# Two layers of linear attention and gated MLP: the sum of the two halves moved to TensorE in the first two tiles, under a newly searched order

## The chip, the cores and the metric

The kernel runs on one core of a Trainium2 chip. A core has TensorE (PE in the profile, with its weight loads as PEld), VectorE (DVE), ScalarE (ACT), GpSimd (POOL) and SyncE (SP), which here only issues transfers; 16 DMA engines move data. TensorE multiplies a stationary block of up to 128x128 with a moving block of up to 512 columns and writes to PSUM. The other engines take their operands from PSUM or from the on-chip memory SBUF. Each engine works through its own list of instructions in order, and waits at an instruction until the semaphores that it names have counted far enough. The metric is the time of one execution on the device, in microseconds (us).

## The reference

The input x has 2048 tokens of 512 channels in bf16. Four stages follow one another, attention A and MLP B, twice, with the same weights:

```
x = x + A(layernorm(x));  x = x + B(layernorm(x));  x = x + A(layernorm(x));  x = x + B(layernorm(x))

A: q, k, v = layernorm(x) @ wqkv            32 heads of 16 channels
   phi(u)  = concat(softmax(u w), softmax(-u w))     per head, w = w_phi
   kv = sum over tokens of phi(k) v^T;  z = sum over tokens of phi(k)
   o  = phi(q) kv / (phi(q) z + 1e-6);  A = o @ wo
B: h  = relu(y @ W_gate) * (y @ W_up)       1376 columns;  B = h @ W_down
```

phi has two halves, one from the softmax of u w and one from that of -u w, so o is a sum of two products, one for each half. Attention is linear: kv and z are sums over all tokens, so the keys of all tiles must be through before the first tile's o can be made.

## The kernel before, in words

The 2048 tokens are 16 tiles of 128. The line numbers are those of the kernel before; in the changed kernel the same code stands 201 lines higher, since a table of numbers became shorter (L867 becomes L666).

For each layer the following is done. Keys, per tile: statistics of x (L810, L811), their logarithm and exponential for the inverse deviation (L818, L820), the normalized tile (L825) and its transpose, by TensorE with an identity and an evacuation for the first tiles, and by a DMA transpose from SP for the others (`turn`, L785 to L805). Then K and V on TensorE (L849, L855), two exponentials on ScalarE (`ek`, L852), their sums per head on VectorE (`sk`, L860), logarithm and exponential of the sums for their inverse (L867, L870), the product phi (L879, on VectorE or GpSimd), and its product with V (`kvz`, L896), which is summed over the 16 tiles in PSUM. From this sum VectorE builds R, the right-hand side of the queries (L918, L924). Queries: TensorE makes Q for four tiles at a time (L937), ScalarE its two exponentials (`Eq`, L941).

Attention, per tile (`attend`, L947): TensorE multiplies Eq with R (`erq`, L955), ScalarE or VectorE copies numerators N and denominators DS out of PSUM, VectorE makes the weights w of the two halves (L971 to L977) and the products pr (L980), adds the two halves to o (L985), o is transposed (`oT`), TensorE projects it (L992), and VectorE adds it to x (L1001). For the first two tiles of a layer the last addition also leaves the row sum of x (L997), so that the centring for the MLP (L1018) doesn't wait for the statistics. In these two tiles transposes are made by TensorE (L797) and evacuated by ScalarE or VectorE; in the others they are DMA transposes.

MLP, per block of one to four tiles (`mlp`, L1006): gate and up on TensorE (L1068, the last 96 columns at L1044), relu and copy out of PSUM (L1072, L752, L753), their product hT (L1076), down on TensorE (L1101) and the addition to x (L1108). The next layer's keys of a tile start when its MLP is done.

Which instruction comes when is not in this text. Every operation is put in a list with its engine, a cost, what it depends on and which buffers it takes. `arrange` and `plan` (L71 on) then go through a model of the five engines and put the instructions in order: of those that can start at the earliest time on an engine, the one with the smallest number in the table DUE goes first. DUE has one number for each operation; it was found by a random search (annealing), not written by hand. A second table of 301 bits, PLACE, says for each PSUM evacuation and each phi product whether it moves to its other engine (ScalarE or VectorE; VectorE or GpSimd). The order is fixed in the built program; at run time the waits alone decide. Where the model has TensorE idle before the first kvz, filler matmuls of zeros are put in (`idle`, L744).

The step that the change touches in `attend` is chosen by a flag:

```
if how == "SP" or not SUM_ON_PE:      # o = pr[0] + pr[1] on VectorE, then turn(o)
else:                                 # turn(pr, parts = its two halves)
```

With two parts, `turn` issues for each of the four blocks of 128 columns two matmuls into the same PSUM columns, the first with start, the second with stop, so that PSUM holds the transposed sum.

Of the kernel before, what the change touches and what calls it, by code (L numbers as in the profile page):

```python
# [226 lines left out]
class K:  # L227
# [9 lines left out]
    "1101000110000001001100001000100000000000010001111000011000010001110001000000000000011100100010111111"  # L237
    "1111000010110100000100000010000001100000011001011000011111100010000100001101010000001001111011010000"
    "1111100110100000010110000100000010100000010011011010100001000001001010001111110011001101111011000111"
# [4 lines left out]
SUM_ON_PE, SPLIT, SUMMED = False, False, 2  # L244
# [6 lines left out]
    124840698555718, 124252925051631, 124840698555715, 125332623046249, 125332623046237, 125332623044945,  # L251
    124563716811943, 124651474002544, 125330408190868, 125332623046304, 124563716811957, 126266507667699,
    125634454115563, 126229628066192, 121775727240306, 126167001450013, 126167001450460, 127129188121561,
    127129188120464, 127094235901023, 126466639653490, 130976565015723, 126315242830809, 126026073780216,
    127094235902555, 127129188121381, 126296162928321, 126296162928067, 124164240787164, 125426364192401,
    125402334135098, 125572680463274, 125519371767392, 125974726071829, 125750504763376, 125579757280012,
    125111116517781, 125262546662859, 123870973169851, 125479091639646, 125519634893654, 125402750569735,
    125720420032606, 126315242829367, 126115429498044, 125777194724969, 125402334135128, 125288327727618,
    125426364192382, 125079834957741, 125262546664085, 125297196294117, 125083742970748, 125572680463271,
    125682458895960, 125340531910116, 125650771760537, 124924227899641, 125375805988896, 125375805988747,  # L260
    125222585690632, 124164240787379, 125079834952887, 125682458896453, 125073457285470, 124441555417783,
    125262546664362, 124559450906168, 125312265963603, 125309490505260, 125650771760388, 125521196029889,
    125302414876135, 125288971855969, 125302414876075, 125319036718893, 125310924577113, 125301244472799,
    125319889098234, 125304622980711, 124441555417022, 124696086271192, 125037102060107, 125289095968268,
    125310342882178, 125097433264852, 123938863413234, 125098635011495, 125302414877679, 125298443103361,
    125302414877834, 125345179807080, 125281974922696, 125170893464912, 125310924577844, 125298773455122,
    124760528650159, 125079834956090, 124164240787032, 125519634912639, 125297196294120, 125289095970570,
    125112530384860, 124947956071454, 125087041208877, 125295339242047, 125295339242044, 125310342881683,
    125302414876836, 125563590222055, 124550413597701, 125170893460583, 125310439811694, 125310924578485,
    125310342891023, 125079834956128, 125059086062919, 125340531910042, 125288971857093, 124938480631522,  # L270
    125016964293686, 125288327733509, 125223398503866, 125345179804453, 125223398503371, 125223398503413,
    128002429020973, 125310342881575, 125004873625443, 125004873624115, 125304250990101, 125307858833262,
    126406478372943, 124715538660738, 125381551257299, 125298773455119, 125309931740009, 125034120871986,
    125223398503145, 124934003878247, 124920547621783, 125117660356287, 125304250989589, 125381551258296,
    125724846491348, 125381551257440, 125381551255756, 124974964922671, 125098650067446, 125291692659804,
    125289095968030, 125289095968469, 125345179805242, 125288327732492, 125098635010687, 125281974923160,
    125307858833059, 125223398502787, 125307858834522, 125140858237361, 126040889629027, 125223398503832,
    125364446854524, 125252231261123, 125381551257841, 125304250990712, 125381551257935, 125172912230709,
    124370185364736, 125108599924050, 125310339518705, 125302251176246, 125291692659817, 116464344164560,
    124922363544296, 125116688267329, 125108599923765, 125310109452139, 125303189236999, 125098650066178,  # L280
    125111066291136, 125026249417504, 125310339519068, 125302251175868, 125301748943397, 125307858834419,
    125262656080157, 125307858833334, 125307858831723, 125281974922936, 125016007547146, 125096908962168,
    125140858236352, 126184070097670, 126789461067573, 124985972327150, 126493631750672, 125298443105832,
    125108599921161, 125095405692172, 124194527561572, 123915330190996, 125076395401661, 125296253501352,
    125034337760696, 125310144379949, 125172912227871, 124207139224249, 123569728375339, 125298628392740,
    125302384093186, 125034337760404, 125310109456339, 125302384093798, 124931075024483, 125294295865377,
    125294295865373, 125302251176101, 125315738277133, 125311054768224, 126406478373023, 125172912230494,
    125096908962530, 125251794872554, 124920547622585, 125303189240357, 125098650068694, 119253338445520,
    125310144376109, 124936451836160, 123979775168383, 123985197582245, 125308558845483, 125268086740942,
    125296661283390, 125310109454666, 125308302113579, 124976494725716, 125154886386050, 125154886386047,  # L290
    125310339518837, 125310339520186, 125311054773229, 115427298652791, 125028606409972, 125308302117330,
    124740066372422, 125309837287326, 124971491447171, 125390463209015, 125414317459497, 124998168317548,
    125310257912136, 125310339399315, 123124172544908, 125030291594481, 125098650066121, 125251794874681,
    125098650067377, 118590723041837, 125302384093189, 118558518521843, 119253338445444, 125315738276049,
    106461658784164, 94447193084223, 125174401625687, 125154442634399, 124740066371701, 125309837288789,
    124971491447250, 125700597007401, 125308302114021, 125724451257015, 125310339520700, 125310339519418,
    125311054772244, 106461658774504, 124207139226908, 125192403773820, 124998168316146, 125311054772195,
    124441758064121, 124971491449373, 125317969331587, 125317969332560, 124974964922433, 121939852109137,
    121830280691129, 125172912227838, 125310144376073, 124836416131697, 125170954590710, 125294295865680,
    125251220555668, 124971491446350, 133210835393138, 125310144376062, 159383179923936, 115427298651984,  # L300
    124869899796944, 121608346900103, 125317969331111, 124895461028154, 124971491450562, 122185707429267,
    122708677636727, 123917343997726, 121939852110706, 123578599439449, 125019087637949, 159383179924917,
    115648665651868, 116063440630281, 125317969332636, 125074078432251, 125317969331341, 123519743654385,
    125310236008505, 120537880156542, 118420113792879, 123578599438633, 121692118966927, 159383179923941,
    159383179924147, 127715336141955, 159383179924206, 127715336141958, 106461658780311, 125332623047314,
    126229643281022, 124563716811954, 124651474004320, 125262546664382, 125310498011902, 125304250992350,
    125345179806077, 125297457021900, 125309490506988, 125310342881875, 125650771760502, 125311152414122,
    125301606200720, 121534934577895, 125301606200572, 125341707123588, 121534934577391, 125311152414125,
    121534934577404, 125652646373752, 125303189240274, 125381551256039, 125304250990207, 125170893460707,
    125170893460683, 125136322776291, 125281974922790, 125098635010684, 125298443103066, 125170893464861,  # L310
# [909 lines left out]
```

The softmax here doesn't subtract the row's maximum and nothing guards it: scores larger than these inputs give would overflow.

## Time and profile before

The time is the median of three runs. The profiled run took 383.81 us, of which the profile spans 382.0.

| | before |
|---|---|
| time, median of 3 (lowest to highest) | 383.95 us (383.66 to 384.04) |
| span of the profiled execution | 382.0 us, 7622 instructions |
| TensorE busy | 371.5 us (97%) |
| VectorE busy | 311.1 us (81%) |
| ScalarE busy | 215.0 us (56%) |
| GpSimd busy | 41.9 us (11%) |
| sum of halves on VectorE (L985) | 32 instructions, 413 ns each |
| transposes of o on TensorE (L797) | 16 matmuls of 128 columns |
| granted TensorE clock | full in all 40 slices |

Busy time is the time in which an engine has at least one instruction under way. Successive instructions of VectorE and ScalarE overlap a little in their records, so that the durations of an engine's instructions add up to more than its busy time. A line of a stretch (A:B) gives its length and then, for each engine, busy us and in brackets the number of instructions. A line of the waits says which engine waited for which engine's line, then us in total, number of waits, and the longest. A line of the timeline gives start and length in us, engine, line, operation, output and inputs, and in square brackets the idle time just before it with what ended it.

### The profile page before, as it was taken

To read this page: it belongs to the slowest core of one execution; us is meant where nothing else is said; L and a number is where in the kernel's file an instruction comes from. 1 tells how busy PE (TensorE), PEld (TensorE's weight loads), DVE (VectorE), ACT (ScalarE), POOL (GpSimd) and SP (SyncE) were. 2 spreads that over 40 slices of the span, in tenths; PEclk is the share of its full clock that TensorE was granted. 3 is DMA by queue.
4 is the path that set the end of the run, shared out by engine and by line. 5 is a ranking of instruction groups with operands and counts; after the bars stand their busy time and mean duration, and the time that the engine had idled before them with its cause. 6 is when DMAs were issued, how large, how long until landed. Compare 5 with 4: busy or idle time off the path is not lost.

```text
span 382.0 us, 7622 instructions
## 1 busy us (share of the span) xinstructions
PE 371.5 (97%) x2787; PEld 224.4 (59%) x2832; DVE 311.1 (81%) x798; ACT 215.0 (56%) x554; POOL 41.9 (11%) x44
## 2 busy tenths in 40 slices
PE   7999998999989999999999999999999999999996
PEld 4545456967545445554656654696855544467575
DVE  7999999999999989983694677999998976763334
ACT  6999989636445316772455679984526412243040
POOL 0276710000200000230020124000000000000000
PEclk9999999999999999999999999999999999999999
DMA  8497720222221321211200100013322221020110
GB/s 232 122 205 219 188 89 2 52 58 62 57 56 41 44 54 40 45 23 27 45 6 15 22 8 1 2 36 70 77 44 70 57 56 56 14 62 16 41 50 29
DMA packets 60869, 22.83 MB, mean 60 GB/s; under 512 B 52672, under 2 KB 59808, under 8 KB 60832
## 3 DMA queue, kind: packets, MB, share of 16 engines
q1 hardware_dynamic: 60416, 21.95, 24.9%
q8 instruction: 22, 0.36, 0.4%
q10 hardware_dynamic: 416, 0.39, 0.4%
q14 instruction: 15, 0.12, 0.1%
HBM read 7.91 MB, written 2.10 MB: 26 GB/s over the span
## 4 chain that ended last, share of the span: by engine, by line
PE 77%; DVE 17%; DMA 2%; issue 2%; ACT 1%; DVEq 0%
PE b L1068 31%; PE b L1101 17%; PE b L855 5%; PE b L849 5%; PE b L992 5%; PE b L937 5%; PE q L955 3%; PE b L1044 2%; PE q L896 2%; DMA xnTA<-xn 2%; DVE pr L980 1%; DVE bstA L810 1%; DVE bstB L810 1%; DVE sk L860 1%; DVE N L753 1%
## 5 line engine op out<-in xcount | busy, mean ns | idle before, releaser
L1068 PE MATMUL b<-xnTB,wgu 128*128 128x128 bf16 (+2 forms) x1191 | 152.3, 279 | 0.5
L1068 PEld LDWEIGHTS <-wgu 128*128 128x128 bf16 x1200 | 97.7, 98 | 42.5
L1072 ACT ACTIVATE gu<-b 128x512 bf16<-128x512 f32 (+1 forms) x83 | 48.0, 584 | 63.7 <-PE b L1068 61.3
L1101 PE MATMUL b<-wd,hT 128*128 128x512 bf16 (+3 forms) x349 | 82.3, 372 | 0.7
L879 POOL TENSOR_TENSOR phiK<-ek,sk 128x512 bf16<-128x512 bf16 x38 | 41.2, 1102 | 192.3 <-ACT sk L870 164.1
L1101 PEld LDWEIGHTS <-hT 128*128 128x128 bf16 (+1 forms) x363 | 34.7, 98 | 33.9 <-DVE hT L1076 0.2
L1076 DVE TENSOR_TENSOR hT<-gu 128x512 bf16<-128x512 bf16 (+1 forms) x83 | 34.0, 414 | 15.4 <-ACT gu L752 14.2
L1108 DVE SCALAR_TENSOR_TENSOR X<-b,rsB,X 128x512 bf16<-128x512 f32 (+1 forms) x33 | 23.7, 729 | 23.8 <-PE b L1101 23.8
L752 ACT CAST gu<-b 128x512 bf16<-128x512 f32 (+1 forms) x50 | 28.4, 570 | 24.0 <-PE b L1068 20.4
L860 DVE TENSOR_REDUCE sk<-ek 128x64 f32<-128x1024 bf16 x32 | 38.6, 1210 | 2.7 <-ACT ek L852 2.3
L852 ACT ACTIVATE ek<-b 128x512 bf16<-128x512 f32 x64 | 36.0, 616 | 8.3 <-PE b L849 8.1
L941 ACT ACTIVATE Eq<-b 128x512 bf16<-128x512 f32 x64 | 37.3, 629 | 3.3 <-PE b L937 3.1
L752 ACT CAST N<-q 128x384 bf16<-128x384 f32 (+1 forms) x59 | 26.1, 464 | 12.4 <-PE q L955 6.7
L855 PE MATMUL b<-wv,xnTA 128*128 128x512 bf16 x123 | 31.9, 379 | 0.3
L937 PE MATMUL b<-xnTA,Wq 128*128 128x512 bf16 x125 | 31.9, 379 | 0.2
L849 PE MATMUL b<-Wk,xnTA 128*128 128x512 bf16 x123 | 31.6, 379 | 0.4 <-DVE xnTA L753 0.2
L992 PE MATMUL b<-wo,oT 128*128 128x512 bf16 x120 | 31.3, 379 | 0.4
L753 DVE CAST gu<-b 128x512 bf16<-128x512 f32 (+1 forms) x33 | 21.8, 665 | 11.1 <-PE b L1068 11.1
L955 PE MATMUL q<-R,Eq 128*128 128x144 bf16 x256 | 27.5, 226 | 1.8 <-DVE N L753 1.3
L955 PEld LDWEIGHTS <-Eq 128*128 128x128 bf16 x256 | 20.3, 98 | 13.1 <-issue 2.6
L980 DVE TENSOR_TENSOR pr<-N,w 128x1024 bf16<-128x1024 bf16 x32 | 21.8, 683 | 0.7
L810 DVE BATCH_NORM_STATS2 bstA<-X 128x6 f32<-128x512 bf16 x32 | 21.3, 682 | 1.2 <-DMA X<-in_A_x_dram 1.0
(75 smaller groups left out, 388.9 us busy)
## 6 DMA issues: line engine op xcount, KB each, us to landing
out_dram<-X SPq DMA_DIRECT2D x15, 128.0 KB, 1.7
X<-in_A_x_dram SPq DMA_DIRECT2D x6, 256.0 KB, 3.3
wgu<-in_B_W_gate_dram SPq DMA_DIRECT2D x4, 344.0 KB, 3.4
wgu<-in_B_W_up_dram SPq DMA_DIRECT2D x4, 344.0 KB, 3.5
wd<-in_B_W_down_dram SPq DMA_DIRECT2D x5, 256.0 KB, 3.5
wv<-in_A_wqkv_dram SPq DMA_DIRECT2D x2, 256.0 KB, 4.7
wo<-in_A_wo_dram SPq DMA_DIRECT2D x4, 128.0 KB, 3.1
oT<-o SPq DMA_TRANSPOSE x28, 2.3
```

Of the source, the lines that this page charges most:

```text
L752: both = {"ACT": ("ACT", act(cols), lambda: nc.scalar.copy(out=out_(), in_=in_()), False), "DVE": ("DVE", dve(cols), lambda: nc.vector.ten ...
L849: k = op("PE", mm(4, 512), due, lambda: [nc.tensor.matmul(kp.t[:], lhsT=xnTA[c][:, b, cols], rhs=Wk2[:, b, :], start=(b == 0), stop=(b == ...
L855: v = op("PE", mm(4, 512), due_v, lambda: [nc.tensor.matmul(vp.t[:], lhsT=xnTA[c][:, b, cols], rhs=wv[:, b, :], start=(b == 0), stop=(b == ...
L860: a = op("DVE", SUM16, due, lambda: nc.vector.tensor_reduce(out=sk.t[:, row, :], in_=ek.t[:].rearrange("p g s (h f) -> p (g s h) f", f=DH) ...
L879: e.tensor_tensor(out=ph.t[:].rearrange("p g s (h f) -> p (g s h) f", f=DH)[:, lo:lo + n], in0=ek.t[:].rearrange("p g s (h f) -> p (g s h) ...
L937: q = op("PE", mm(4, 512), due(c, b), lambda b=b, qp=qp: [nc.tensor.matmul(qp.t[:], lhsT=Wq2[:, m, b * P:(b + 1) * P], rhs=xnTA[c][:, m, : ...
L941: done.append(op("ACT", act(512), due(c, b), lambda b=b, s=s, qp=qp: nc.scalar.activation(out=Eq[c][:, b, s, :], in_=qp.t[:], func=AF.Exp, ...
L955: pe.append(op("PE", mm(len(groups), GE), due, lambda ps=ps, groups=groups: [nc.tensor.matmul(ps.t[:, n * GE:(n + 1) * GE], lhsT=Eq[c][:, ...
L992: a = op("PE", mm(4, 512), due + 3, lambda: [nc.tensor.matmul(yp.t[:], lhsT=oT.t[:, b, :], rhs=wo[:, b, :], start=(b == 0), stop=(b == NB ...
L1068: nc.tensor.matmul(ps.t[:, q * W:(q + 1) * W], lhsT=wgu[:, s, b, g * P:(g + 1) * P], rhs=xT.t[:, b, 0:W], start=(b == 0), stop=(b == NB - 1))
L1072: nc.scalar.activation(out=gu.t[:, 0, 0:cols], in_=gp.t[:, 0:cols], func=AF.Relu)
L1101: nc.tensor.matmul(yp.t[:, 0:c1 - c0], lhsT=h.t[:m, f * W + i * P:f * W + (i + 1) * P], rhs=wd[:m, f, c0:c1], start=(f == 0), stop=(f == N ...
```

## The change

SUM_ON_PE becomes true. SUMMED, the number of tiles with the row sum, is 2 in both kernels. PLACE and DUE are replaced by the result of another search, which began from nothing and was short; there are 2101 numbers for 2105, because four additions are gone. The numbers serve for comparison only, so their size means nothing.

```
-    "1101000110000001001100001000100000000000010001111000011000010001110001000000000000011100100010111111"
+    "0000000100000000001000000010000010000000100000110100111010110000110000100000010001000110001101010101"
...
-SUM_ON_PE, SPLIT, SUMMED = False, False, 2
+SUM_ON_PE, SPLIT, SUMMED = True, False, 2
...
 DUE = (
-    124840698555718, 124252925051631, 124840698555715, 125332623046249, 125332623046237, 125332623044945,
...
+    140234, 138986, 141443, 132421, 137184, 136724,
 )
```

In the built programs the instructions of before and after differ in number as follows: additions L985 on VectorE 32 and 28, transposing matmuls L797 56 and 72, filler matmuls 13 and 15, phi products 26 and 29 on VectorE (38 and 35 on GpSimd), evacuations of V 10 and 6 on VectorE (22 and 26 on ScalarE), and smaller shifts of the same kind. On every engine the order is a different one throughout.

## The prediction

> **What bounds the kernel now.** I read the page first, then the waits of TensorE, then tables by stretch, then the timeline where TensorE stands still.
>
> ```profile
> span 382.0 us, 7622 instructions
> PE 371.5 (97%) x2787; PEld 224.4 (59%) x2832; DVE 311.1 (81%) x798; ACT 215.0 (56%) x554; POOL 41.9 (11%) x44
> ...
> 16.00:48.00 32.00, 31.74 (x213) 15.67 (x216) 30.94 (x55) 30.97 (x89) 21.94 (x22) 1.00 0.81 207
> 48.00:54.00 6.00, 5.95 (x69) 3.60 (x69) 5.58 (x14) 5.00 (x14) 0.92 (x1) 1.00 0.39 130
> 54.00:64.00 10.00, 8.40 (x71) 4.96 (x70) 9.03 (x30) 9.83 (x31) 0.00 (x0) 1.00 0.00 0
> 64.00:100.00 36.00, 35.79 (x369) 27.06 (x371) 35.69 (x116) 20.28 (x57) 0.00 (x0) 1.00 0.27 57
> ...
> PE q L955 <- DVE N L753: 1.3, 2, 1.1
> ...
> PE b L797 <- DVE o L985: 1.0, 2, 0.6
> ```
>
> The columns of the stretch lines are busy TensorE, weight loads, VectorE, ScalarE and GpSimd. TensorE is full, but not alone: from 16 to 48 us (layer 0's keys and values) VectorE and ScalarE are full as well, and to 100 us VectorE still is. Only from 160 us on has TensorE room on all sides. It loses time in few places: 54 to 64 us, where the first attention tiles go through, is the largest with 1.6 us.
>
> To see where exactly, I put a ledger beside the trace. TensorE's work is its matmuls in order at the rate of four of 512 columns in 0.86 us; it comes to 369.9 us. Start time less work done is 4.5 at 12 us, 4.6 at 44, 6.0 at 59, 7.45 at 62.5, 7.3 at 99, 8.5 at 107, 8.4 at 233, 9.0 at 238 and 8.8 at the end; 3.3 us follow the last matmul. So 369.9 + 8.8 + 3.3 = 382.0, the span of the profiled run (383.81 timed; the three others have the median 383.95). The steps at 53 to 62 us (2.6), 107 us (1.2) and 237 us (0.6) are what an order can win or lose; the rest is start and tail.
>
> The timeline shows the first step:
>
> ```profile
> 56.14 0.18 ACT L752 COPY DS<-q 128x32 f32<-128x32 f32 x1
> ...
> 56.54 0.22 DVE L971 TENSOR_TENSOR m<-DS 128x64 f32<-128x64 f32 x1
> ...
> 57.74 0.69 DVE L980 TENSOR_TENSOR pr<-N,w 128x1024 bf16<-128x1024 bf16 x1
> ...
> 58.47 0.42 DVE L985 TENSOR_TENSOR o<-pr 128x512 bf16<-128x512 bf16 x1
> ...
> 58.95 0.40 PE L797 MATMUL b<-ident,o 128*128 128x128 bf16 x4 [0.59 <-DVE o L985]
> ...
> 59.38 0.59 ACT L752 CAST oT<-b 128x512 bf16<-128x512 f32 x1
> ...
> 60.02 1.04 PE L992 MATMUL b<-wo,oT 128*128 128x512 bf16 x3
> ...
> 63.86 1.95 PE L1068 MATMUL b<-xnTB,wgu 128*128 128x128 bf16 x32
> ```
>
> One chain: ScalarE's copy of tile 0's sums, five small VectorE steps, the product, the sum of halves, the transpose, its evacuation, the projection; 3.9 us from 56.1 to 60.0.
>
> **What the Trainium skill says.** "TensorE: Matmul & The Clock Gate", part on the extra over 53.3 ns, puts warm matmuls of 128 and 512 columns back to back at 55.6 and 215.7 ns; the trace agrees: four of 512 in 0.86 us, and 72 of 128 in the 4.18 us from 367.25, 58 each. The same page's step on LDWEIGHTS says that only weight loads are pulled ahead and matmuls keep program order, and its table calls ScalarE's and VectorE's queues strict FIFO. So one early instruction that waits holds all behind it; the trace has VectorE's o holding the transposes of L797 and they the erq matmuls behind them. "VectorE: DVE Perf Modes", tier table, gives tensor_tensor on bf16 in SBUF 1224 ns for 2048 elements; no instruction here has that length, and the row of L985 has 413 ns for 512, which I use.
>
> **The change part by part.** The row sum with the residual (L997) stands in both kernels for t below 2, so this half changes nothing. The sum on TensorE takes four adds from VectorE, 4 x 413 ns = 1.65 us, and gives TensorE 16 more matmuls of 128 columns, 16 x 56 ns = 0.9 us. Two more filler matmuls (15 for 13) add 0.43 us, in waits at the start. TensorE's work becomes 371.2. Placement moves a net 2.1 us onto ScalarE, and with the adds gone some 2 us off VectorE. SP issues 101 transposes in both. All this is small. What matters is that nearly every instruction stands in another place.
>
> For that I extend the ledger to VectorE and ScalarE: mean durations of before's rows, less the overlap of successive records (VectorE's records sum to 360.1 us against 311.1 busy, 0.06 each; ScalarE's to 260.1 against 215.0, 0.08 each). Time less work is then, in before, 2.8 for VectorE from 12 to 48 us, and for ScalarE 4.0 at 16 us and 2.0 at 60.
>
> Step 1, keys of layer 0. ScalarE's logarithm (L867) waits for VectorE's sum (L860). In before ScalarE's ledger stands at 19.9 where VectorE's must stand at 20.8 (its tightest, 0.9 apart), and at 41.1 for 39.9. In after it is 13.5 for 15.2, 16.8 for 18.7, and 41.1 for 41.9. With VectorE 2.8 late, the last pair starts ScalarE at 41.9 + 2.8 + 0.1 = 44.8, where before's ScalarE stood at 41.1 + 2.0 = 43.1. So ScalarE is held by 1.6 us. Bounds: 0 (VectorE earlier by as much) and 3 (what both wait for each other adds up).
>
> Step 2, attention entrance. Tile 0's DS and N copies end at ScalarE's ledger 54.0 and 54.3 in before, 56.1 and 56.4 in after: more of the queries' exponentials (L941, 0.63 us each) go ahead. Without step 1: copy at 56.1 + 2.0 = 58.1, m at 58.2, pr done 1.9 later at 60.1, transposes at once (saving the add's 0.42), 8 in 0.46, done 60.65. Evacuation ends 61.4, projection 61.5 to 62.4, residual 63.2, centring 63.85, transpose 63.9 to 64.3, evacuation 65.05; the second tile's projection runs beside it. First gate/up matmuls start 65.7, with 57.6 us of TensorE's ledger done; in before 63.86, with 56.4. What remains is equal (313.6 and 313.5), so 1.85 us later is 1.85 us longer. With step 1 TensorE's offset is 65.7 - 57.6 + 1.6 = 9.7.
>
> Step 3, VectorE-bound stretch to about 130 us. TensorE must wait where VectorE's ledger leads its own most: before +4.4 at TensorE's 127 (offset 8.35, so VectorE's own is 4.0); after +4.3 at 123. After's m starts at 59.8 with step 1, at ledger 53.3: VectorE is 6.5 late, before 3.9. That makes 10.8 at most; it makes 9.7 if VectorE needs no more than it gets. I take 10.3.
>
> Step 4, layer 1's entrance. First erq stands 1.75 us of TensorE work behind the last kvz in both (wait 0.6 as before). The add saves its 0.42, mostly hidden; the centred tile's transpose stands 0.9 us of work behind the projection instead of 1.7, where 1.3 is needed: 0.4 more. Drift as before -0.2. I take +0.7. Bounds 0 and 1.5.
>
> Transfers: a K at TensorE's 25.1 needs a DMA transpose whose source VectorE makes 1.0 before it in the ledger; the tightest of before is 1.5, with a wait of half a microsecond. That costs up to 0.5, which step 2's ScalarE hides. Tail: the last G/U group is followed by 18 half-width down matmuls (25 mixed in before); the last chunk's copies and product end just before their turn. No change.
>
> Sum: 371.2 + 10.3 + 0.7 + 3.3 = 385.5 of span, 3.5 over before; 383.95 + 3.5 gives 387.4.
>
> **The rivals.** First, not slower: the saved add pays. Place: the transposes of L797 at both entrances; price: 4 x 0.42 = 1.7 off the chains, less 0.9 of TensorE, gives 383.2. It decides if the first gate/up matmul starts by 63.9. For it: the waits on o are TensorE's own. Against: ScalarE, not the add, sets when tile 0's chain starts. Chance 0.13.
>
> Second, worse: in the keys' stretch VectorE waits for ScalarE's exponentials (L852) and ScalarE for VectorE's sums, and each loses what the other lost. If 16 tiles lose 0.2 us each, 3.2 on top of mine: 390.6. For it: three engines at 97% or more leave no slack. Against: the leads grow no further after 18.8. Chance 0.19.
>
> Third, within the main case: VectorE's 2 us less work gives step 3 back, 386.8. I count it there.
>
> **How the numbers follow.** Main case 0.68, at 385.0 to 389.5. A measurement tells about 0.2%, 0.77 us. Below 383.2 lies half of the first rival, 0.06; within 0.2% the other half and an edge of mine, 0.08; slower 0.86. The range leaves out most of the first rival and the upper end of the second: 384.6 to 391.5.
>
> **What would show it.** Step 1: ScalarE's logarithms (L666 in after) wait for the sums more than the 5.7 us of before, and busy ScalarE in 16 to 48 us falls below 30. Step 2: first gate/up matmuls at 66 to 68 us. Step 3: TensorE waits 0.5 us or more on VectorE between 100 and 140 us. Step 4: about a microsecond lost near 240. From 145 to 235 no loss. I am wrong if gate/up starts by 64, or if much is lost after 145.

## The result, and the profile after

The changed kernel takes 387.19 us (median of 4 runs, 386.94 to 388.83), the kernel before, measured beside it, 383.81 (4 runs, 383.61 to 384.04). The ratio is 1.0097, 95% interval 1.0069 to 1.0126: slower by about 1%. The profiled execution spans 385.4 us, 3.4 more than before; 387.4 and 385.5 were predicted.

The head of the page and the stretches, in the columns of the prediction, and below them the stretch from 100 us in before:

```profile
span 385.4 us, 7717 instructions
PE 376.9 (98%) x2850; PEld 225.3 (58%) x2850; DVE 306.6 (80%) x795; ACT 220.2 (57%) x556; POOL 40.7 (11%) x41
...
16.00:48.00 32.00, 30.61 (x213) 14.92 (x212) 30.77 (x53) 30.80 (x87) 16.15 (x15) 1.00 0.93 196
54.00:64.00 10.00, 8.82 (x77) 5.03 (x74) 7.89 (x25) 9.60 (x25) 0.00 (x0) 1.00 0.00 0
...
100.00:160.00 60.00, 59.91 (x356) 30.61 (x355) 56.11 (x161) 29.92 (x75) 4.23 (x4) 1.00 0.25 52
```
```profile
100.00:160.00 60.00, 58.61 (x353) 30.85 (x357) 57.44 (x153) 29.39 (x77) 2.43 (x3) 1.00 0.23 45
```

TensorE's busy time is longer overall; part of that is that the trace of before lacks 45 records of matmuls (2787 for 2832 weight loads). And yet TensorE is idle where it was not before: 1.4 us of the 32 in the keys of layer 0, against 0.3. The last two columns are the share of time in which the DMA engines were busy, and GB/s; in the keys the share is 0.93 for 0.81 before. Between 100 and 160 us, where before lost 1.4, it now stands still for 0.1.

In 20 to 50 us no matmul of before waits for anything; one weight load waits for a transpose:

```profile
PEld L855 <- DMA xnTA<-xn: 0.5, 1, 0.5
```

The waits of the changed kernel's matmuls there, then the queue of SP and TensorE's timeline around the longest:

```profile
PE b L648 <- DMA xnTA<-xn: 1.4, 2, 1.1
```
```profile
25.59 0.58 SPq L473 DMA_DIRECT2D wgu<-in_B_W_up_dram  x1
26.21 0.43 SPq L473 DMA_DIRECT2D wgu<-in_B_W_gate_dram  x1
26.74 1.19 SPq L586 DMA_TRANSPOSE xnTA<-xn  x1
```
```profile
29.42 0.67 PE L695 MATMUL q<-vext,phiK 128*128 128x65 bf16 x16
31.22 1.04 PE L648 MATMUL b<-Wk,xnTA 128*128 128x512 bf16 x4 [1.13 <-DMA xnTA<-xn]
```

K of a tile waits until 31.22 us for a transpose that SP issued at 26.74, directly behind two weight loads. The loads take 4.1 and 4.4 us to land, so they are there at about 29.7 and 30.6, and the transpose lands behind them, at 31.2. The detail of the tile xnTA gives the time from issue to landing of layer 0's twelve transposes, first in before, then in the changed kernel:

```profile
DMA to landing us min/median/max: 2.4/3.1/4.1
```
```profile
DMA to landing us min/median/max: 2.4/3.5/5.4
```

The chain through the first tile, as the prediction showed it for before:

```profile
59.33 0.18 ACT L551 COPY DS<-q 128x32 f32<-128x32 f32 x1
...
59.72 0.23 DVE L770 TENSOR_TENSOR m<-DS 128x64 f32<-128x64 f32 x1
...
60.93 0.69 DVE L779 TENSOR_TENSOR pr<-N,w 128x1024 bf16<-128x1024 bf16 x1
...
61.67 0.62 PE L596 MATMUL b<-ident,pr 128*128 128x128 bf16 x8
...
62.33 0.59 ACT L551 CAST oT<-b 128x512 bf16<-128x512 f32 x1
...
62.97 1.04 PE L791 MATMUL b<-wo,oT 128*128 128x512 bf16 x4 [0.22 <-ACT oT L551]
...
66.82 2.40 PE L867 MATMUL b<-xnTB,wgu 128*128 128x128 bf16 x40
```

From ScalarE's copy to the projection it takes 3.6 us (before 3.9): the add is gone. But the chain begins 3.2 us later, and gate/up at 66.82 instead of 63.86.

The prediction's offset (start time of a matmul less TensorE work done) shows where the loss lies. The two middle versions are experiments told below:

| TensorE work done, us | before | sum alone, old order | weight loads last | changed |
|---|---|---|---|---|
| 20 | 4.3 | 4.2 | 4.5 | 4.6 |
| 27 | 4.55 | 4.2 | 4.5 | 5.9 |
| 46, end of the keys | 4.6 | 4.5 | 5.2 | 6.5 |
| 58, first gate/up | 7.4 | 6.75 | 7.9 | 9.2 |
| 95 | 7.15 | 6.5 | 8.1 | 9.0 |
| 112 | 8.3 | 7.7 | 8.3 | 9.2 |
| 220 | 8.4 | 7.7 | 8.35 | 9.4 |
| 242, layer 1's entrance | 9.1 | 8.3 | 9.8 | 10.8 |
| end | 8.8 | 7.9 | 9.8 | 10.9 |
| work | 369.9 | 370.8 | 371.2 | 371.2 |
| span | 382.0 | 382.1 | 384.3 | 385.4 |

Changed against before: work +1.3; keys +1.9; the step from the keys to the first gate/up about the same (2.7 for 2.8); the step at 100 us gone (-0.9 by 112 us of work); +0.1 to 220; layer 1's entrance +0.7; +0.4 behind it. That is 3.4.

### The profile page after: what moved, and what is told of

It is laid out like the page before. It is cut to its first block, busy times and chain, and to the rows that moved or that the text cites. A ratio compares the mean times of both kernels' runs of the same rounds, so it can differ in the third digit from the quotient of the medians.

```text
span 385.4 us, 7717 instructions
## 1 busy us (share of the span) xinstructions
PE 376.9 (98%) x2850; PEld 225.3 (58%) x2850; DVE 306.6 (80%) x795; ACT 220.2 (57%) x556; POOL 40.7 (11%) x41
## 4 chain that ended last, share of the span: by engine, by line
PE 81%; DVE 13%; DMA 2%; issue 2%; ACT 1%; SPq 0%; DVEq 0%; ACTq 0%
PE b L867 34%; PE b L900 18%; PE b L791 6%; PE b L654 4%; PE b L648 4%; PE b L736 4%; PE q L754 3%; PE b L843 2%; DVE sk L659 2%; DVE bstA L609 2%; PE q L695 2%; DMA xnTA<-xn 1%; DVE pr L779 1%; PE b L596 1%; PE q L545 1%
## 5 line engine op out<-in xcount | busy, mean ns | idle before, releaser
L900 PE MATMUL b<-wd,hT 128*128 128x512 bf16 (+2 forms) x363 | 85.6, 373 | 0.0
L678 POOL TENSOR_TENSOR phiK<-ek,sk 128x512 bf16<-128x512 bf16 x35 | 40.0, 1159 | 194.4 <-ACT sk L669 142.6
L651 ACT ACTIVATE ek<-b 128x512 bf16<-128x512 f32 x64 | 34.8, 597 | 15.3 <-PE b L648 15.0
L551 ACT CAST gu<-b 128x512 bf16<-128x512 f32 (+1 forms) x51 | 29.3, 574 | 23.5 <-PE b L867 23.3
L740 ACT ACTIVATE Eq<-b 128x512 bf16<-128x512 f32 x64 | 36.1, 611 | 1.4 <-PE b L736 1.0
L791 PE MATMUL b<-wo,oT 128*128 128x512 bf16 x128 | 32.5, 379 | 0.2 <-ACT oT L551 0.2
L551 ACT CAST N<-q 128x384 bf16<-128x384 f32 (+1 forms) x57 | 25.3, 460 | 9.1 <-PE q L754 6.8
L552 DVE CAST gu<-b 128x512 bf16<-128x512 f32 (+1 forms) x32 | 21.0, 657 | 7.0 <-PE b L867 6.7
L678 DVE TENSOR_TENSOR phiK<-ek,sk 128x512 bf16<-128x512 bf16 x29 | 21.8, 775 | 1.3 <-ACT sk L669 1.2
```

The lines of the kernel that those rows point to most:

```text
L551: both = {"ACT": ("ACT", act(cols), lambda: nc.scalar.copy(out=out_(), in_=in_()), False), "DVE": ("DVE", dve(cols), lambda: nc.vector.ten ...
L678: e.tensor_tensor(out=ph.t[:].rearrange("p g s (h f) -> p (g s h) f", f=DH)[:, lo:lo + n], in0=ek.t[:].rearrange("p g s (h f) -> p (g s h) ...
L740: done.append(op("ACT", act(512), due(c, b), lambda b=b, s=s, qp=qp: nc.scalar.activation(out=Eq[c][:, b, s, :], in_=qp.t[:], func=AF.Exp, ...
L791: a = op("PE", mm(4, 512), due + 3, lambda: [nc.tensor.matmul(yp.t[:], lhsT=oT.t[:, b, :], rhs=wo[:, b, :], start=(b == 0), stop=(b == NB ...
L900: nc.tensor.matmul(yp.t[:, 0:c1 - c0], lhsT=h.t[:m, f * W + i * P:f * W + (i + 1) * P], rhs=wd[:m, f, c0:c1], start=(f == 0), stop=(f == N ...
```

## The experiments

All but one of these kernels keep the text of the one kernel or the other and give each engine its instructions in a list, so that single instructions can be moved:

```diff
+    line = {e: sorted((o for o in ops if o.eng == e), key=lambda o: o.due) for e in HOP}
...
             for o in cand:
+                if o is not line[e][0]:
+                    continue
```

Without a move, every instruction stands where it stood. In them the lines lie 14 higher up than in the changed kernel: K is L634, the transposes on TensorE L582, erq L740, gate/up L853. "Before" is measured beside each group on the same chip.

**The sum alone, in the old order.** Order and placement of the kernel before; only the four adds go.

```diff
-SUM_ON_PE, SPLIT, SUMMED = False, False, 2
+SUM_ON_PE, SPLIT, SUMMED = True, False, 2
```

> The sum on TensorE alone: every engine keeps the order and placement of the kernel before, only the four adds (L985, first two tiles of each layer) are taken out and the transposes sum the halves. Theory one (the loss of the change is in the new order, the sum is worth next to nothing): TensorE gets 0.9 us more, each entrance loses up to two adds of 0.42 from its chain, so 383.2 to 384.5 us, within 0.2% of before. Theory two (the sum itself costs, by 16 more matmuls and longer transposes in the chain): 384.8 to 386.

384.08 us against 383.9, ratio 1.0004 (0.9996 to 1.0012): no difference. TensorE's work grows by 0.9 us, and its waits shrink by as much (7.9 for 8.8 at the end), more than half of it in the first entrance, where two waits on o (1.0 us) give way to transposes that start as soon as pr is there:

```profile
58.37 0.62 PE L582 MATMUL b<-ident,pr 128*128 128x128 bf16 x8
```

The flag therefore neither costs nor brings anything here. The 3.4 us come with the new order and its placement.

**The new order without the sum.** The four adds come back, each directly behind its pr on VectorE; else the changed kernel's order.

```diff
-SUM_ON_PE, SPLIT, SUMMED = True, False, 2
+SUM_ON_PE, SPLIT, SUMMED = False, False, 2
```

> The new order alone: order and placement of the changed kernel, with the four adds put back on VectorE right behind their products and single transposes. Theory one (order): 386.3 to 388 us, as slow as the changed kernel within 0.3%. Theory two (the sum itself costs): 385.5 us or less.

391.01 us, ratio 1.0187 (1.0174 to 1.0200): 3.8 more than the changed kernel, and above both windows. This order has TensorE come to the transposes when pr is due, so it waits for each of the four adds. The waits of the whole execution:

```profile
PEld L582 <- DVE o L770: 3.0, 4, 0.9
...
PE b L582 <- DVE o L770: 2.0, 4, 0.7
PEld L777 <- DMA oT<-o: 1.1, 1, 1.1
```

0.9 us of the 3.8 lie in the keys, which the adds do not touch (see the repetition below). The rest, some 3 us, is more than the four adds themselves take (1.65 us); what makes up the difference is not taken apart here. What the saved adds are worth depends on the order: nothing in one, some 3 us in the other.

**Two weight loads behind the transpose that K waited for.**

```diff
 SP: transpose xn -> xnTA                (issued at 24.35 us in the changed kernel)
-SP: load W_up, load W_gate
 SP: transpose xn -> xnTA                (26.74 us)
+SP: load W_up, load W_gate
```

> The changed kernel with one edit on SP: the two weight loads (W_up and W_gate, 344 KB each) issued at 25.6 and 26.2 us go behind the DMA transpose of the normalized tile that was issued after them at 26.7, whose landing the K matmuls waited for until 31.2 us (1.3 us lost). All else keeps its order. Transfer theory: the transpose lands in 2.4 to 3.1 us instead of 4.4, the K matmuls start by 30.2, and the kernel gains 0.9 to 1.3 us: 385.9 to 386.3. Rival, as I predicted it (ScalarE is held by VectorE's sums and hides the transfer): the wait goes but the first gate/up matmul still starts at 66.4 to 66.9, and the time stays at 387.0 to 387.4.

387.21 us, ratio 1.0094 (1.0078 to 1.0111): no gain. The moved transpose now lands in 2.4 us and K does not wait for it. But other transposes hold TensorE:

```profile
PE b L634 <- DMA xnTA<-xn: 1.8, 2, 1.5
```

The longest of these waits ends at 40.26 us. Its transpose was issued at 34.53, directly behind another weight load (issued at 33.85), and took 5.7 us. The same transpose held K in the changed kernel too, by 0.26 us. The profiled execution was the slowest of the five (388.79), so the wait is shown for it alone.

**The old order for the keys, the new one from the first erq on.** The 386 operations that the kernel before starts ahead of its first erq come in its order, all others in the changed kernel's.

```diff
-order = new
+order = [o for o in old if it is ahead of the old first erq] + [the rest, as in new]
```

> The changed kernel, but all that the kernel before issues ahead of its first erq matmul (386 operations: set-up, keys of layer 0, the first queries) stands in the order and placement of before; what follows stands in the order of the changed kernel. If the loss of 1.7 us in the keys (TensorE's time less work at 46 us of work: 6.5 against 4.8), with two fillers fewer, is kept to the end: 384.9 to 385.5. If another engine then binds and gives it back (VectorE up to 130 us, as my step 3 had it): 386.3 or more.

388.3 us, ratio 1.0113 (1.0097 to 1.0129). The keys were restored (offset 4.6 at 49 us of work), and all of it was lost again by the first gate/up (9.7), at 66.97 us instead of 66.82. In ScalarE's timeline seven exponentials of the queries stand ahead of tile 0's copies:

```profile
55.03 3.54 ACT L726 ACTIVATE Eq<-b 128x512 bf16<-128x512 f32 x7 [0.64 <-PE b L722]
58.39 0.25 ACT L537 COPY DS<-q 128x32 f32<-128x32 f32 x1
```

I took this at first for support of the prediction's second step (ScalarE sets the entrance). It is not: at the seam of the two orders all Q matmuls run ahead of the first erq, so the erq matmuls have nothing to fill their waits. In both kernels 8 or 12 of the Q matmuls stand between the first erq matmuls. TensorE's clock falls here too (see the last section), but that does not show in the time: in three of the four runs the mean granted clock is 0.995 or 0.996, and the fourth has 1.0 at the same time (388.29 us). The next group avoids seams.

**All weight loads behind the transposes.** Only SP's queue changes.

```diff
-SP: 7 loads of W_gate/W_up, 4 of wo, among the transposes
 SP: the last transpose xn -> xnTA of layer 0
+SP: 4 loads of wo, 7 of W_gate/W_up
 SP: 6 loads of W_down
```

> The changed kernel with one queue reordered: on SP's queue the seven gate/up weight loads (all but the first) and the four wo loads move behind the last xn transpose; no other engine's order moves. In the trace of the changed kernel TensorE lost 1.9 us more than before by the end of the keys, 1.3 of it at 31.2 us where K waited for a transpose that two weight loads were queued ahead of. Theory A, the transfers carry the loss: TensorE's offset at the end of the keys falls from 6.5 to about 4.6 to 5 and the time to 385.3 to 386.0. Theory B, ScalarE's order carries it (it was held 6.5 us by VectorE's key sums and reaches tile 0's copies late whatever K does): the transfer wait goes, another takes its place before the first gate/up, which stays at 66.2 to 66.9 us, and the time stays at 386.8 to 387.5. If the loads come too late for their users, a wait on the weights shows at 60 to 70 us and the time is above 388.

386.42 us against 384.09, ratio 1.0058 (1.0046 to 1.0071), and the span is 384.3. Against the changed kernel (1.0097) that is a gain of 1.5 us by the ratios and of 1.1 us by the spans. The DMA share of the stretch falls from 0.93 to 0.50, and the transposes land sooner:

```profile
16.00:48.00 32.00, 31.65 (x229) 15.93 (x228) 31.72 (x55) 31.28 (x89) 16.65 (x15) 1.00 0.50 118
```
```profile
DMA to landing us min/median/max: 2.4/2.6/4.6
```

In 20 to 50 us no matmul waits for a transpose any more; the only wait of a matmul there is this one:

```profile
PE q L681 <- POOL phiK L664: 0.3, 1, 0.3
```

The gain goes through: the offset is 1.3 less at the end of the keys, 1.25 less at the first gate/up, and 1.1 less at the end. The first gate/up starts at 65.57:

```profile
65.57 2.40 PE L853 MATMUL b<-xnTB,wgu 128*128 128x128 bf16 x40
```

Theory B named 6.5 us for which ScalarE's logarithms wait for VectorE's sums. That is a total over the whole execution (before 5.7, here 6.3), and nearly all of it lies behind 56 us. In 16 to 48 us, the keys of layer 0, the waits are these, in before, in the changed kernel and here:

```profile
ACT sk L867 <- DVE sk L860: 0.4, 2, 0.2
```
```profile
ACT sk L666 <- DVE sk L659: 0.6, 1, 0.6
```
```profile
ACT sk L652 <- DVE sk L645: 0.3, 1, 0.3
```

So ScalarE was hardly held in the keys, and the transfers carried most of the loss. The time came 0.4 above theory A's window, because 0.6 of the 1.9 is lost in the keys for other reasons, 0.35 of it by a kvz matmul that waits for GpSimd's phi at 40.8 us.

**Two copies of tile 0 ahead of one exponential**, in the changed kernel and together with the loads:

```diff
 ACT: Eq
+ACT: DS and N of tile 0
 ACT: Eq (the last ahead of them)
-ACT: DS and N of tile 0
```

> The changed kernel with ScalarE's two copies of tile 0's DS and N moved ahead of one exponential of the queries, and nothing else. As the prediction had it, these copies set when tile 0's product is formed: then the first gate/up starts about 0.7 us earlier and the time falls by 0.4 to 0.7, to about 386.6. As the trace of the changed kernel reads, VectorE's own copy of N ends at the same instant (59.70 us), after waiting for TensorE: then nothing moves by more than 0.2 and the time is 387.1 to 387.3.

> The two reorderings together (weight loads behind the transposes, the two ScalarE copies ahead of one exponential). If transfers and ScalarE each hold the entrance within some tenths of each other, only both together bring the gain: 385.0 to 385.6, with each alone at 386.5 or more. If the transfers carry it alone, the same as the loads moved alone, within 0.2. If neither, 387.2.

388.82 us (ratio 1.0119, 1.0106 to 1.0133) alone, and 386.61 (1.0064, 1.0051 to 1.0078) with the loads last, where 386.42 was without the copies. The clean pair is the second: not faster, and its entrance costs 2.95 us instead of 2.7. ScalarE is through with the two copies at 58.38 us, but VectorE with its own of N only at 58.47, so m starts at 58.50, as without the move (58.47); and the copies of the next sums, which now follow two exponentials, come later, so that erq waits longer for their buffers:

```profile
59.90 0.77 PE L740 MATMUL q<-R,Eq 128*128 128x144 bf16 x5 [0.78 <-ACT DS L537]
```

against 0.48 without. ScalarE's copies do not set tile 0's chain.

**The changed kernel once more.** The copies alone had cost 1.6 us, but 1.26 of it in the keys, ahead of the edit.

> The changed kernel once more, unaltered. The version that differs from it only behind 57 us (two copies ahead of one exponential) had already lost 7.7 us by the end of the keys, against 6.5 in the profile of the changed kernel, and its runs lay 1.6 us higher. If the transfers of the keys make the time of this order vary from run to run, this profile's offset at the end of the keys lies between 6 and 8 and again goes with its time, and the runs spread over more than 1 us, where the version with the loads last spread over 0.4. If the two copies themselves cost the 1.6 us, the runs lie at 386.9 to 387.5 and the offset at 6.5.

388.1 us (386.95 to 388.44, ratio 1.0096, 1.0082 to 1.0110), and in this profile the transposes hold TensorE longer:

```profile
PEld L648 <- DMA xnTA<-xn: 2.8, 3, 1.8
...
PE b L648 <- DMA xnTA<-xn: 1.7, 1, 1.7
```

Four profiled executions with this order of the keys (the changed kernel twice, the version with the two copies, that with two loads moved) lost 6.5, 6.9, 7.7 and 7.9 us by their end; they took 387.19, 387.81, 388.95 and 388.79. This order of the keys is slower and less steady: the changed kernel's runs spread over 1.9 and 1.5 us, those with the loads last over 0.4 and those with the old keys and the new rest over 0.5. It is when the transposes land that varies; why it varies from run to run, these runs do not show.

**One load ahead of one transpose, in the old order.** The converse of the second try, on the order of the kernel before with the sum.

```diff
 SP: transpose xn -> xnTA                (23.34 us)
 SP: load x
+SP: load W_up
 SP: transpose xn -> xnTA                (25.25 us)
```

> The order of the kernel before with the sum on TensorE (384.1), and one weight load (344 KB) put ahead of one xn transpose on SP's queue, the transpose that K reads some 3.9 us after its issue; the changed kernel had two loads right ahead of the same transpose and K waited 1.25 us. If a load ahead of a transpose costs what the changed kernel lost: TensorE waits 0.3 to 1.2 us for that transpose, the time is 384.4 to 385.2. If the lead of 3.9 us covers it: no wait, 384.0 to 384.2.

384.35 us (ratio 1.0012, 1.0004 to 1.0020) where 384.08 was without it, in another group; this lies between the two windows. In the profiled execution (384.03) the offset rises by about 0.15 at 24 to 27 us of work and no more. The transpose, now issued at 25.98, takes 3.4 us, and its K starts at 29.44, as soon as it has landed: one load used up the room that there was. In the changed kernel, with two loads ahead, the time from issue to use would have been 3.35 (issued 26.74, due 31.22 - 1.13 = 30.09), and the transpose took 4.4.

**One wait of the old order.** TensorE waits 1.06 us for VectorE's copy of N at 107 us; two gate blocks go ahead of it.

```diff
-PE: erq (2 matmuls), G (4), down (3), G (4)
+PE: G (4), G (4), erq (2 matmuls), down (3)
```

> The order of the kernel before with the sum on TensorE (which took 384.1), and one move on TensorE's queue: the two matmuls for queries at about 107 us, which wait 1.06 us there for VectorE's copy of N, and a down block behind them go behind the next two gate blocks. If that wait is time lost (the trace of the changed kernel has none there, and 1.2 us less loss between 100 and 160 us), the time falls by 0.8 to 1.1, to about 383.1. If the wait only moves to the next operation that needs VectorE, it stays at 384.0 to 384.3.

383.68 us against 384.09, ratio 0.9988 (0.9981 to 0.9994), between the two windows. It is the fastest of all these kernels, by a tenth of a per cent. The wait is gone:

```profile
106.10 1.89 PE L853 MATMUL b<-xnTB,wgu 128*128 128x512 bf16 x8
107.83 0.29 PE L740 MATMUL q<-R,Eq 128*128 128x144 bf16 x2
```

At 95 us of work the offset is 6.9, and it stays there past the place where the old order loses 1.2; then it rises by 0.6 until 118, so half is given back. A wait taken out of a stretch in which VectorE is near its limit is here half passed on; a new order of the whole stretch, as the changed kernel has, loses 0.1 there.

**Layer 1's entrance**, exchanged at about 217 us: the old order with the sum, then the new one; and the new order with the loads last, then the old one.

```diff
-order = old                     | -order = new, loads last
+order = old, from 216 us new    | +order = new, loads last, from 218 us old
```

> The order of the kernel before with the sum on TensorE (384.1) up to some 216 us, and from there the changed kernel's order: layer 1's entrance to attention alone is the new one. In the traces TensorE's offset rises there by 1.4 us in the changed kernel and by 0.5 with the old order. If that step belongs to the new order of this stretch: 384.8 to 385.3. If it comes from what the earlier stages left behind: 384.0 to 384.3.

> The changed kernel with the weight loads behind the transposes (386.4) up to some 218 us, and from there the order of the kernel before. If the step at layer 1's entrance belongs to the new order of that stretch: 385.3 to 385.7. If it was left by the earlier stages: 386.2 to 386.6.

386.27 (ratio 1.0064, 1.0051 to 1.0076) and 386.86 (1.0073, 1.0060 to 1.0087). Both times miss every window, because the seams themselves cost 0.8 and 1.6 us; in the second it is this wait:

```profile
PE b L582 <- DVE xn L610: 1.2, 1, 1.2
```

Behind the seams the steps can be read: from 220 to 242 us of work the offset rises by 1.4 in the first (8.7 to 10.1) and by 0.6 in the second (10.35 to 10.9). The changed kernel has 1.4, before 0.7, and the sum alone 0.6. The step goes with the order of this stretch, whatever came before it. This is read from one profile each, not from the times, and which waits make up the step is not taken apart.

## Why the prediction was right, and where it was not

Time, sign and span were met, but in part by luck: errors cancelled, and a loss that the prediction held to be small stood in for one that was not there.

- *TensorE's work.* 371.2, as predicted. That 16 more matmuls cost what the saved adds bring is shown by the sum alone.
- *Step 1, keys: this step failed.* ScalarE was to be held by 1.6 us by VectorE's sums (44.8 less 43.1 is 1.7). The sign that was named, waits of more than 5.7 us, came out (6.5), but it is a total over the whole execution; in 16 to 48 us the waits are 0.6, and before 0.4. Busy ScalarE did not fall below 30 (30.80). With the transposes out of the way the offset at the first gate/up is 7.9, only half a microsecond above before's 7.4, where 9.7 was predicted.
- *The transfers: this step failed.* It was "costs up to 0.5, which step 2's ScalarE hides". The transposes cost not up to a half but 1.3 us, more in other executions, and nothing hid it: with the loads moved away, 1.25 came back at the first gate/up. I had compared positions in the order (1.0 for 1.5) and not what else was in the queue; no matmul had waited for a transpose in 20 to 50 us before, but that the lead was enough there said nothing of an order with a shorter lead and other loads beside it.
- *Step 2, entrance.* Gate/up at 66.8 lies in the window of 66 to 68, and the offset, 9.2, near the 9.7. The way there was wrong, and that it came near is luck: the 1.3 us of the transposes stand where the 1.6 us of step 1 were. The entrance costs about 2.7 us in both kernels; it begins later since the keys end later. ScalarE's copies, which were to set it, do not: earlier, they gain nothing.
- *Step 3, VectorE's stretch.* +0.6 was predicted and a wait of half a microsecond between 100 and 140 us. There is none, and before's own 1.2 there is gone as well. Perhaps VectorE's ledger, summed from mean durations, overstated what its engine needs in a new order; that was not tested. This was the third rival's "gives step 3 back", and more than it allowed.
- *Step 4, layer 1's entrance.* +0.7 for a measured 1.4, within the bound of 1.5.
- *Sum.* 0.5 too much at the entrance and 0.4 more in step 3 stand against 0.8 too little from step 4 on: 10.9 us of offset for 11.0.

Of the rivals, "the saved add pays" is refuted for the old order (0.9 saved, 0.9 paid) and true in the new one, where the sum is worth some 3 us and is still not enough. The mutual waits of VectorE and ScalarE did not come: of the keys' 1.9 us, 1.3 go with the transfers and 0.35 are a wait for GpSimd, and ScalarE's logarithms wait there for 0.6 us in all.

## What to carry to other kernels

Before a saved instruction is credited, look whether the order has its consumer standing there: the same four adds were worth nothing and 3 us. A transfer's lead is to be judged with what is queued and under way beside it, and the cheap test is to move all other loads behind, since with two moved another transpose held TensorE. A wait has to be read in the stage that it is to explain: a total over the whole execution hid that ScalarE hardly waited in the keys. A sum that meets the time is no proof of its terms; the terms need their own experiments, and exchanging whole stretches between two orders costs a seam that has to be read apart.

## What the runs showed of the hardware

Layer 0's twelve transposes, of one size and from one queue, took 2.4 us from issue to landing at best, and at most 4.1, 5.4 and 4.6 us in three orders of the same transfers. The Trainium skill, "DMA: Bandwidth & Descriptors", section "Two DMAs through the same engine are not ordered", says that within one queue of an engine descriptors start in order. That fits a transpose that lands behind the two loads issued ahead of it, and in 2.4 us when they are issued behind it; no run here shows single descriptors. Whether the order of the queue holds the transpose, or the loads' share of the DMA engines, is not separated: moving the loads changes both. Nor is it the weight loads alone, for with all of them issued behind, one transpose still took 4.6 us.

In the kernel with the old keys and the new rest TensorE's clock was halved without TensorE ever having stood still for long. Its stretches, with the granted clock third from the end:

```profile
54.00:57.00 3.00, 3.00 (x19) 1.56 (x18) 0.72 (x3) 2.36 (x6) 0.00 (x0) 1.00 0.00 0
57.00:60.00 3.00, 1.12 (x11) 0.65 (x9) 2.31 (x9) 3.00 (x10) 0.00 (x0) 1.00 0.00 0
60.00:61.00 1.00, 0.86 (x11) 0.64 (x11) 0.75 (x3) 0.92 (x4) 0.00 (x0) 0.93 0.00 0
61.00:64.00 3.00, 2.92 (x16) 1.53 (x15) 1.94 (x7) 1.44 (x5) 0.00 (x0) 0.50 0.00 0
```

```profile
62.17 1.89 PE L777 MATMUL b<-wo,oT 128*128 128x512 bf16 x4
```

Four matmuls of 512 columns took 1.89 us instead of 1.04. The Trainium skill, "TensorE: Matmul & The Clock Gate", Part 1, gives half clock after an idle window of about 3.4 us. Here the clock began to fall between 60 and 61 us. In the three microseconds to 60 TensorE was busy for 1.12, ahead of them without a break, and the longest wait was 0.63 us. In this execution a run of short waits was enough; how few would be, was not tried.
